# Attention scores of two heads at once: keys and queries transposed in float32 and split afterwards, scores as two 64-row tiles in three passes, one pool of PSUM banks

## The chip, the cores and the metric

The kernel runs on one core of a Trainium2 chip. The metric is the device time of one execution in microseconds (us). Five engines work side by side, each through its own instructions in a fixed order: TensorE (PE; its weight loads are listed apart as PEld), VectorE (DVE), ScalarE (ACT), GpSimd (POOL) and SyncE (SP), which issues most of the DMAs. TensorE writes only to PSUM, which the kernel uses as 8 banks of 128 partitions by 512 float32 values.

## The reference

```python
B, H, S, D = 4, 8, 576, 64
scores = np.matmul(q, k.transpose(0, 1, 3, 2)) / np.sqrt(D)
kth = np.partition(scores, -32, axis=-1)[..., -32:-31]        # the 32 largest of each row stay
scores = np.where(scores >= kth, scores, -1e9)
attn = softmax(scores)
x = (attn @ v)            # laid out as 2304 tokens of 512
# a mixture of experts on x: each token goes to the expert (of 8) with the largest logit
h = relu(x[mask] @ w1[e]); y[mask] = gate[mask] * (h @ w2[e])     # 512 -> 1024 -> 512
# a second block on y: SoLU, a normalization, and w_out
h = y @ w_in; s = h * softmax(h); out = normalize(s) * g_ln @ w_out
```

The scores must keep float32's exactness, since a row's 32nd largest decides which entries stay. A float32 value v is therefore written as hi + lo, where hi is v rounded to the type float32r, which TensorE multiplies in one pass, and lo is the rest; q.k is then a sum of products of such parts.

## The kernel before, in words

The kernel is one long program without loops on the chip. It is written as some twenty generators (load_k, load_q, prep_k_all, prep_q_all, attention with unit, pair and route, slots with front, backs with back and moe2, statics for the weights of the last block). Each yields its operations, with an engine and an estimated cost in ns, and takes and returns tokens of buffers ("get", "put"). A planner (class Order, L97) runs these against each other with the estimated costs and priorities (PRI, L35) and so fixes each engine's order of instructions before the program is built. On the chip every engine takes its instructions in that order; only the semaphores decide when.

Attention goes by batch b (4), tile t of queries (four of 128 rows, then one of 64) and pair p of heads (4). For the 128-row tiles a unit is one head (128 units), for the 64-row tile a unit is both heads of a pair, stacked as 128 rows (16 units).

- prep_kv (L481) makes a pair's keys ready: ACT copies the raw keys to hi (L486), POOL subtracts to lo (L487), TensorE transposes nine blocks of 128 by 128 in which hi and lo of one head lie side by side (L507), and ACT copies them out of PSUM in three pieces (L513). The result holds hi in partitions 0 to 63 and lo in 64 to 127.
- prep_q (L520) and turn_q (L535) do the same for queries: ACT (L527) and POOL (L528) split half a tile at a time, TensorE makes four transposes per pair (L543) and ACT copies each pair out (L549; for the 64-row tile L555, with zeros from POOL at L554). For one head there are two stationary operands of 128 rows: (hi, lo) and (lo, hi).
- unit (L563) makes the scores: both operands against the keys' (hi, lo), for two halves of 288 keys, so four matmuls of 128 rows and 288 columns a head (L579), eight for the stacked 64-row unit, in two PSUM banks. ACT copies both halves out (L586, L595), DVE takes the larger and the smaller of the halves (L597, L598) and then finds the 32nd largest by rounds of MAX8 and MATCH_REPLACE8 (L601 to L615). ACT and POOL make the masked exponentials (L632 to L636).
- pair (L645) transposes the exponentials (L668, L680, L683) and multiplies them with v (L702), in column tiles of 64.
- The experts are at L971 and L1002, the last block at L1023, L901 and L1084. A slot of 128 tokens becomes ready when enough rows of attention have been routed (PLAN, L53).

PSUM: all tiles share eight banks, and the planner hands them out by four kinds of token: pS = 2 for scores, T = 2 for transposes, O = 1 for the product with v, P = 3 for the last block and the experts. pS and O go to P when attention is done.

DMAs of k, q, v and the experts' weights are all issued by SP, in the planned order; an issue that waits for its buffer holds up those behind it. The buffer of raw keys (kr) and that of raw queries (qr) exist once each, transposed keys four times (kT), transposed queries twice (qT, one pair each).

Of the kernel before, what the change touches and what calls it, by code (L numbers as in the profile page):

```python
# [32 lines left out]
TUNE = dict(kr=1, qr=1, hl3=1, khl=1, kT=4, vt=6, qT=2, S=5, M=2, e=2, tops=5, eT=2, eT4=1, oT=1, xs=3, z=8, seq=1,  # L33
            row=2, xT=2, yT=4, tile=4, wraw=5, hh=2, tT=4, u=1, ot=2, pS=2, T=2, O=1, P=3, unit=7, pair=6)
# [9 lines left out]
OB = "O"  # L44
# [148 lines left out]
def attn_moe_solu_kernel(ctx, tc, q, k, v, mid, w_gate, mbias, w1, w2, w_in, w_out, g_ln, out):  # L193
# [12 lines left out]
    BUF = dict(kr=2, qr=2, hl3=1, khl=1, kT=4, vt=4, qT=3, S=SBUFS, M=2, e=3, tops=4, eT=2, eT4=1, oT=1, xs=2, z=8, seq=1,  # L206
               row=3, xT=2, yT=6, tile=4, wraw=6, ws=4, hh=2, tT=4, u=2, ot=2, pS=2, T=2, O=1, P=3, unit=UNITS, pair=2)
# [56 lines left out]
    def consts():  # L264


        yield "get", ("row", 2), ("xs", 1), ("T", 1)
# [40 lines left out]
        yield "put", ("T", 1)  # L308
# [57 lines left out]
    def static_w_in(kk, i, j):  # L366
# [4 lines left out]
        yield "get", ("P", 1)  # L371
# [4 lines left out]
        yield "put", ("P", 1)  # L376

    def static_w_out(kk, j):
# [3 lines left out]
        yield "get", ("P", 1 if pm else 2)  # L382
# [5 lines left out]
        yield "put", ("P", 1)  # L388
# [11 lines left out]
    def static_centre():  # L400
# [8 lines left out]
        yield "put", ("P", 1)  # L409
        done = [Ev() for _ in range(KF)]  # L410

        def centre(kk):
# [3 lines left out]
            yield "get", ("P", 1)  # L416
# [5 lines left out]
            yield "put", ("P", 1)  # L422
# [57 lines left out]

    def prep_kv(b, p):  # L481
        yield k_loaded[b, p]
        kr = kraw[b, p]
        yield "get", ("khl", 1)
        khl = sb.tile([128, 9, 2, D], F32R, tag="khl", name="khl", bufs=BUF["khl"])
        yield Op("ACT", 573, lambda: nc.scalar.activation(khl[:, :, 0, :], kr, AF.Copy))  # L486
        yield Op("POOL", 1360, lambda: nc.gpsimd.tensor_tensor(khl[:, :, 1, :], kr, khl[:, :, 0, :].bitcast(F32),  # L487
                                                               op=OP.subtract))
        yield "put", ("kr", 1)
# [10 lines left out]
        kt = sb.tile([128, 2, S], F32R, tag="kT", name="kT", bufs=BUF["kT"])  # L500
        for c0, c1 in ((0, 4), (4, 8), (8, 9)):
            yield "get", ("T", 1)
            pt = ps.tile([128, 4, 128], F32R, tag="B", name="pt", bufs=8)

            def tr():
                for c in range(c0, c1):
                    nc.tensor.transpose(pt[:, c - c0, :], khl[:, c, :, :].rearrange("p a d -> p (a d)"), identr)  # L507

            yield Op("PE", 60 * (c1 - c0), tr)
            at, w = ((0, 512), (640, 512), (512, 128))[c0 // 4]  # L510
            if c0 == 8:
                yield "put", ("khl", 1)
            yield Op("ACT", 478 if c0 < 8 else 157, lambda: nc.scalar.activation(  # L513
                kt.rearrange("p s n -> p (s n)")[:, at:at + w], pt[:, :c1 - c0].rearrange("p i n -> p (i n)").bitcast(F32), AF.Copy))
# [949 lines left out]
```

## Time and profile before

| | |
|---|---|
| three runs | 1073.13, 1073.67, 1076.36 us; median 1073.67 |
| the profiled execution | 1071.05 us, of which the span of its instructions is 1069.2 |
| busy over the span | PE 88%, PEld 75%, DVE 74%, ACT 68%, POOL 61% |
| chain that ended last | PE 56%, DVE 11%, DMA 9%, POOL 8%, ACT 5% |
| TensorE's granted clock, mean | 0.964 |

Busy is the share of the span in which an engine had an instruction under way; a matmul's end is modelled, and matmuls overlap, so a matmul's duration is longer than the distance from its start to the next one's. That distance is read from the starts in the timeline. The chain is followed back from the last instruction: at each step to what released it, or to the instruction before it on its engine. "x" is the number of instructions.

### The profile page before, as it was taken

The page shows a single profiled execution, that of the slowest core. Times are in us where ns is not written, and L with a number is a line of the kernel's source. Part 1 is how long each engine was busy: PE and PEld are TensorE (multiplying, and loading weights), DVE is VectorE, ACT ScalarE, POOL GpSimd, SP SyncE. Part 2 cuts the span into 40 slices and gives each one's busy share as a digit, 9 for nine tenths or more (in the row PEclk, how much of TensorE's full clock was granted, in tenths as well). Part 3 has the DMA queues.
Part 4 walks back from the last instruction along what each step waited for, and adds up shares of the span by engine and source line. Part 5 has one row for each costly group of instructions (what it writes and reads, how often), then busy time and mean ns, then how long its engine had stood idle before and what let it go on. Part 6 is the DMA issues. An engine that isn't in the chain of part 4 may idle for free.

```text
span 1069.2 us, 22944 instructions
## 1 busy us (share of the span) xinstructions
PE 942.3 (88%) x7230; PEld 800.8 (75%) x7230; DVE 787.9 (74%) x2717; ACT 731.9 (68%) x1798; POOL 649.5 (61%) x1397
## 2 busy tenths in 40 slices
PE   4677678988998989989999989999999979899993
PEld 3444456867887878878887878888888858788882
DVE  5988898975989989978899978888999721632111
ACT  5868676777787878868878767888787732533231
POOL 5768765775657767666677765766776534641111
PEclk9889898999999999989999989999999999999997
DMA  4443414336432434435433444244443337434530
GB/s 120 138 149 99 103 54 125 92 105 142 119 112 71 111 97 120 139 91 148 113 88 77 133 111 145 81 114 81 145 105 101 100 82 168 148 109 138 163 116 13
DMA packets 141243, 119.30 MB, mean 112 GB/s; under 512 B 31900, under 2 KB 113976, under 8 KB 141112
## 3 DMA queue, kind: packets, MB, share of 16 engines
q1 hardware_dynamic: 137016, 107.69, 37.6%
q0 software_dynamic: 4096, 10.05, 3.0%
q8 instruction: 59, 0.97, 0.4%
q14 instruction: 72, 0.59, 0.3%
HBM read 105.50 MB, written 12.21 MB: 110 GB/s over the span
## 4 chain that ended last, share of the span: by engine, by line
PE 56%; DVE 11%; DMA 9%; POOL 8%; ACT 5%; issue 4%; POOLq 0%; ACTq 0%; DVEq 0%
PE ph L971 10%; PE py L1002 9%; PE po L1084 8%; PE ph L1023 6%; DMA wraw<-in_moe_w_dram 6%; PE po L702 6%; PE pS L579 5%; PE pt L668 4%; DVE M L605 2%; POOL e L634 2%; PE pt L901 2%; PE pt L543 2%; DMA xg<-xrows,ids 2%; PE px L711 1%; DVE tops L608 1%
## 5 line engine op out<-in xcount | busy, mean ns | idle before, releaser
L634 POOL TENSOR_TENSOR e<-ss,e 128x576 f32<-128x576 f32 x144 | 206.3, 1436 | 52.1 <-ACT e L633 47.3
L605 DVE MATCH_REPLACE8 M<-tops,M 128x288 f32<-128x288 f32 x432 | 190.4, 442 | 0.0
L971 PE MATMUL ph<-xT,wraw 128*128 128x128 f32 x1088 | 152.5, 286 | 22.2 <-DMA wraw<-in_moe_w_dram 19.3
L971 PEld LDWEIGHTS ph<-xT,wraw 128*128 128x128 f32 x1088 | 138.5, 198 | 29.2 <-issue 13.1
L1002 PE MATMUL py<-hh,wraw 128*128 128x128 f32 x1088 | 147.4, 279 | 1.2 <-ACT hh L981 1.2
L636 ACT ACTIVATE e<-e,nb 128x576 f32<-128x576 f32 x144 | 112.1, 778 | 39.3 <-POOL e L634 38.4
L1002 PEld LDWEIGHTS py<-hh,wraw 128*128 128x128 f32 x1088 | 134.6, 193 | 5.4 <-issue 1.8
L579 PE MATMUL pS<-kT,qT 128*128 128x288 f32 x640 | 127.5, 326 | 10.3 <-ACT qT L549 9.0
L633 ACT ACTIVATE e<-ss,bt 128x576 f32<-128x576 f32 x144 | 111.0, 775 | 31.1 <-POOL bt L632 29.6
L608 DVE MAX8 tops<-M 128x8 f32<-128x288 f32 x288 | 128.5, 447 | 1.1
L702 PE MATMUL po<-eT,vt 128*64 128x128 f32 (+3 forms) x1600 | 115.2, 276 | 15.1 <-ACT eT L672 12.5
L1084 PE MATMUL po<-wo,lT 128*128 128x512 f32 x432 | 122.3, 420 | 3.6 <-ACT lT L905 2.1
L1023 PE MATMUL ph<-wi,yT 128*128 128x512 f32 x432 | 115.7, 407 | 2.0 <-ACT yT L1184 2.0
L702 PEld LDWEIGHTS po<-eT,vt 128*64 128x64 f32 (+1 forms) x1600 | 82.5, 138 | 43.7 <-ACT eT L672 15.8
L579 PEld LDWEIGHTS pS<-kT,qT 128*128 128x128 f32 x640 | 97.7, 199 | 21.1 <-ACT qT L549 9.6
L597 DVE TENSOR_TENSOR M<-pS,ss 128x288 f32<-128x288 f32 x144 | 64.4, 448 | 45.2 <-ACT ss L595 44.6
L672 ACT ACTIVATE eT<-pt 128x512 f32<-128x512 f32 (+1 forms) x160 | 88.2, 553 | 13.6 <-PE pt L668 12.2
L1084 PEld LDWEIGHTS po<-wo,lT 128*128 128x128 f32 x432 | 78.3, 195 | 21.6 <-DVE lT L909 3.0
L668 PE MATMUL pt<-identr,e 128*128 128x128 f32 (+1 forms) x640 | 92.6, 269 | 0.3 <-ACT ss L586 0.2
L1023 PEld LDWEIGHTS ph<-wi,yT 128*128 128x128 f32 x432 | 76.1, 188 | 20.9 <-ACT yT L1184 3.0
L981 ACT ACTIVATE hh<-ph 128x128 f32<-128x128 f32 (+1 forms) x144 | 40.1, 279 | 68.2 <-PE ph L971 67.6
L668 PEld LDWEIGHTS pt<-identr,e 128*128 128x128 f32 (+1 forms) x640 | 72.2, 142 | 11.4 <-issue 4.4
(218 smaller groups left out, 1951.4 us busy)
## 6 DMA issues: line engine op xcount, KB each, us to landing
wraw<-in_moe_w_dram SPq DMA_DIRECT2D x288, 256.0 KB
xrows<-xs SPq DMA_DIRECT2D x16, 288.0 KB
raw<-in_moe_w_out_dram SPq DMA_DIRECT2D x8, 512.0 KB
kr<-in_k_dram SPq DMA_DIRECT2D x32, 128.0 KB
qr<-in_q_dram SPq DMA_DIRECT2D x16, 256.0 KB
vt<-in_v_dram SPq DMA_DIRECT2D x32, 128.0 KB
raw<-in_moe_w_in_dram SPq DMA_DIRECT2D x8, 512.0 KB
wstage<-da SPq DMA_DIRECT2D x8, 256.0 KB
```

The costliest lines, as they stand in the source:

```text
L579: nc.tensor.matmul(pS[hf], w, kt[:, l, hf * HALF:(hf + 1) * HALF], start=i == 0, stop=i == 2 * len(srcs) - 1)
L605: nc.vector.match_replace(out=M, in_to_replace=rounds[r], in_values=M, imm_value=NEG)
L608: nc.vector.max(rounds[r + 1], M)
L633: yield Op("ACT", 667, lambda: nc.scalar.activation(e, ss, AF.Relu, bias=bt, scale=-BIG))
L634: yield Op("POOL", 1360, lambda: nc.gpsimd.tensor_tensor(e, ss, e, op=OP.subtract))
L636: yield Op("ACT", 760, lambda: nc.scalar.activation(e, e, AF.Exp, bias=nb, scale=0.125, accum_out=z))
L668: nc.tensor.transpose(pt[:, c, :], ef[r, at:at + 128], ident[r, r])
L702: nc.tensor.matmul(po[hs, :n], w, x, start=c == 0, stop=c == 4)
L971: nc.tensor.matmul(ph[:, :n], a[:, kk * 128:(kk + 1) * 128], b[:, kk, c0:c0 + n], start=kk == 0 and i == 0, stop=kk == KD - 1 and i == len ...
L1002: nc.tensor.matmul(py[c // k_][:, c % k_, :n], a[:, c * 128:(c + 1) * 128], b[:, :n], start=first and m == 0 and c % k_ == 0 and i == 0, s ...
L1023: nc.tensor.matmul(ph, y[a][:, kk, :], wi[b][:, kk, i * 512:(i + 1) * 512], start=kk == 0 and j == 0, stop=kk == KD - 1 and j == 2)
L1084: nc.tensor.matmul(po, l[a][:, c, :], wo[b][:, kk, :], start=kk == 0 and j == 0, stop=kk == KF - 1 and j == 2)
```

## The change

1. Keys (prep_kv): the load puts the two heads of a pair side by side, so that one float32 transpose turns 64 dimensions of both heads into 128 partitions: head 0 in 0 to 63, head 1 in 64 to 127. Four such transposes fill one bank and one more, of 64 rows, does the last 64 keys. The split comes after: ACT copies hi out of PSUM, DVE subtracts hi from PSUM and writes lo. The last 64 keys are written twice, ahead of and behind the 512, so that head 0 reads its 576 keys from column 64 and head 1 from column 0. The buffer of raw keys is returned after the last transpose; before, after the split.
2. Queries (prep_q): a whole tile, four pairs, in one bank by four float32 transposes, one split by ACT and DVE (for the 64-row tile two of each, and POOL writes the zeros). The buffer qT, still two, now holds a whole tile.
3. Scores (new function scores): for a 128-row tile both heads of a pair at once, as two 64-row tiles of the array, hi.hi, hi.lo and lo.hi: twelve matmuls in four banks. For the 64-row tile six matmuls of 128 rows in two banks. The second head's unit waits for the first one's operation.
4. PSUM tokens: one kind, B = 8, in place of pS, T, O and P. A token sc lets one pair at a time collect its banks.

```diff
-TUNE = dict(kr=1, qr=1, hl3=1, khl=1, kT=4, vt=6, qT=2, ..., pS=2, T=2, O=1, P=3, unit=7, pair=6)
+TUNE = dict(kr=1, qr=1, kT=4, vt=6, qT=2, ..., B=8, sc=1, unit=7, pair=6)
...
-                        nc.sync.dma_start(kr[:, 4 * s:4 * s + 4, :], k[b, 2 * p + s, 0:512].rearrange("(p c) d -> p c d", c=4))
-                    nc.sync.dma_start(kr[:, 8, :], k[b, 2 * p:2 * p + 2, 512:576, :])
+                        nc.sync.dma_start(kr[:, s:8:2, :], k[b, 2 * p + s, 0:512].rearrange("(p c) d -> p c d", c=4))
+                    nc.sync.dma_start(kr[0:64, 8:10, :], k[b, 2 * p:2 * p + 2, 512:576, :].rearrange("s p d -> p s d"))
...
+    def parts_of(hi, lo, pt, n):
+        yield Op("ACT", 55 + n * 833 // 1000, lambda: nc.scalar.activation(hi, pt, AF.Copy))
+        yield Op("DVE", 70 + n * 1042 // 1000, lambda: nc.vector.tensor_tensor(lo, pt, hi.bitcast(F32), op=OP.subtract))
...
     def prep_kv(b, p):
-        yield Op("ACT", 573, lambda: nc.scalar.activation(khl[:, :, 0, :], kr, AF.Copy))
-        yield Op("POOL", 1360, lambda: nc.gpsimd.tensor_tensor(khl[:, :, 1, :], kr, khl[:, :, 0, :].bitcast(F32), op=OP.subtract))
-        yield "put", ("kr", 1)
...
+        kt = sb.tile([128, 2, 640], F32R, tag="kT", name="kT", bufs=BUF["kT"])
+        yield "get", ("B", 1)
+        pt = ps.tile([128, 4, 128], F32, tag="B", name="pt", bufs=8)
+        def tr():
+            for c in range(4):
+                nc.tensor.transpose(pt[:, c, :], kr[:, 2 * c:2 * c + 2, :].rearrange("p s d -> p (s d)"), ident)
+        yield Op("PE", 440, tr)
+        yield from parts_of(kt[:, 0, 64:576], kt[:, 1, 64:576], pt.rearrange("p c n -> p (c n)"), 512)
+        yield "put", ("B", 1)
+        yield "get", ("B", 1)
+        pl = ps.tile([128, 64], F32, tag="B", name="pt", bufs=8)
+        yield Op("PE", 110, lambda: nc.tensor.transpose(pl, kr[0:64, 8:10, :].rearrange("p s d -> p (s d)"), ident[0:64, 0:64]))
+        yield "put", ("kr", 1)
+        ends = kt.rearrange("p a (e n) -> p a e n", n=64)[:, :, 0:10:9, :]
+        yield from parts_of(ends[:, 0], ends[:, 1], bc(pl, 2, 1), 128)
...
     def prep_q(b, t):
+        yield "get", ("qT", 1), ("B", 1)
+        x = qT[b, t] = sb.tile([128, 2, NP, 128], F32R, tag="qT", name="qT", bufs=BUF["qT"])
+        pt = ps.tile([128, NP, n], F32, tag="B", name="pt", bufs=8)
+        def tr():
+            for p in range(NP):
+                nc.tensor.transpose(pt[:, p, :], qr[:n, 2 * p:2 * p + 2, :].rearrange("p s d -> p (s d)"), ident[:n, :n])
+        yield Op("PE", 440, tr)
+        yield "put", ("qr", 1)
+        if n == 128:
+            yield from parts_of(x[:, 0], x[:, 1], pt, NP * n)
...
+    def scores(b, t, p):
+        n = rows_of(b, t)[1]
+        x, kt = qT[b, t], kT[b, p]
+        yield "get", ("sc", 1)
+        yield "get", ("B", 2)
+        if n == 128:
+            yield "get", ("B", 2)
+        bank = [[ps.tile([128, HALF], F32, tag="B", name="pS", bufs=8) for _ in range(2)] for _ in range(n // 64)]
+        yield "put", ("sc", 1)
+        def mm():
+            for i, (a, c) in enumerate(((0, 0), (0, 1), (1, 0))):
+                for hf in range(2):
+                    for s in range(n // 64):
+                        r = slice(64 * s, 64 * s + 64) if n == 128 else slice(0, 128)
+                        at = 64 * (1 - s) + hf * HALF
+                        nc.tensor.matmul(bank[s][hf], x[r, a, p, :], kt[r, c, at:at + HALF], start=i == 0, stop=i == 2)
+        yield Op("PE", 900, mm)
...
     def unit(b, t, p, s, abt, tht, u, no, done):
+        if not s:
+            yield q_ready[b, t]
+            yield kv_ready[b, p]
+            yield from scores(b, t, p)
+        yield scored[b, t, p]
+        pS = pS_[b, t, p][s or 0]
         yield "get", ("S", 1)
-        yield "get", ("pS", 2)
...
-        yield "put", ("pS", 2)
+        yield "put", ("B", 2)
```

Everywhere else "T", "O" and "P" in a get or a put become "B"; the two puts that gave pS and O to P at the end of attention are gone. In pair, the columns of the exponentials that are read for a 64-row tile start at 0 for both heads, since both now see their keys in one order.

## Rows read from the trace of the kernel before

**Rows 1.** Busy us by stretch (windows): stretch, length, each engine's busy time (instructions), PEclk, DMA share, GB/s.
```profile
0.00:175.00 175.00, 116.81 (x654) 79.13 (x654) 145.85 (x458) 126.52 (x285) 122.73 (x185) 0.91 0.39 111
175.00:850.00 675.00, 642.35 (x5332) 561.49 (x5333) 588.62 (x2115) 532.94 (x1349) 452.36 (x1025) 0.98 0.42 110
850.00:1069.00 219.00, 183.10 (x1245) 160.19 (x1245) 53.45 (x146) 72.43 (x165) 74.44 (x188) 0.96 0.42 118
```
**Rows 2.** PE's waits, 0 to 175 us: us in total, times, longest.
```profile
PE pt L507 <- POOL khl L487: 9.8, 2, 8.4
PE pS L579 <- ACT qT L549: 9.0, 3, 3.9
PE pt L543 <- POOL qhl L528: 5.5, 2, 3.5
```
**Rows 3.** DVE's longest wait, 175 to 850 us.
```profile
DVE M L597 <- ACT ss L595: 35.8, 39, 5.7
```
**Rows 4.** Groups by line on PE and PEld: instructions, busy us, mean ns, idle before.
```profile
L543 PE MATMUL pt<-identr,qhl 128*128 128x128 f32 x256 | 35.3, 265 | 5.5 <-POOL qhl L528 5.5
L543 PE MATMUL pt<-identr,qhl 64*128 64x64 f32 x64 | 8.0, 247 | 0.1
L507 PE MATMUL pt<-identr,khl 128*128 128x128 f32 x144 | 22.0, 269 | 9.8 <-POOL khl L487 9.8
L668 PEld LDWEIGHTS pt<-identr,e 64*128 64x128 f32 x128 | 10.3, 140 | 4.6 <-issue 2.4 <-ACT kT L513 0.3 <-ACT ss L586 0.2
```
**Rows 5.** PE's timeline around 424 us: start us, us, line, tiles, rows*columns of the array.
```profile
420.22 1.28 PE L579 MATMUL pS<-kT,qT 128*128 128x288 f32 x8
421.33 0.60 PE L668 MATMUL pt<-identr,e 128*128 128x128 f32 x4
421.86 0.50 PE L543 MATMUL pt<-identr,qhl 64*128 64x64 f32 x4
422.29 1.66 PE L1084 MATMUL po<-wo,lT 128*128 128x512 f32 x6
423.79 0.60 PE L668 MATMUL pt<-identr,e 128*128 128x128 f32 x4
424.22 1.06 PE L971 MATMUL ph<-xT,wraw 128*128 128x128 f32 x8
425.12 1.06 PE L1002 MATMUL py<-hh,wraw 128*128 128x128 f32 x8
425.93 0.54 PE L507 MATMUL pt<-identr,khl 128*128 128x128 f32 x4
426.30 1.29 PE L579 MATMUL pS<-kT,qT 128*128 128x288 f32 x8
```
**Rows 6.** PE's timeline around 455 us.
```profile
454.34 0.46 PE L668 MATMUL pt<-identr,e 64*128 64x64 f32 x4
454.73 1.16 PE L971 MATMUL ph<-xT,wraw 128*128 128x128 f32 x8
455.81 0.46 PE L711 MATMUL px<-iw,oT 128*64 128x144 f32 x2
```
**Rows 7.** PE's timeline in the 9 ns from 445.336 to 445.345 us.
```profile
445.34 0.33 PE L683 MATMUL pt<-identr,e 128*64 128x128 f32 x2
```
**Rows 8.** Groups by line on PE, 175 to 850 us: the scores.
```profile
L579 PE MATMUL pS<-kT,qT 128*128 128x288 f32 x536 | 100.7, 315 | 0.0
```
**Rows 9.** Groups by line on ACT.
```profile
L549 ACT ACTIVATE qT<-pt 128x512 fp32r<-128x512 f32 x64 | 38.3, 598 | 2.5 <-PE pt L543 2.2 <-PE pt L507 0.2
L527 ACT ACTIVATE qhl<-qr 128x512 fp32r<-128x512 f32 x32 | 20.4, 638 | 0.0
```
**Rows 10.** Groups by line on POOL.
```profile
L528 POOL TENSOR_TENSOR qhl<-qr,qhl 128x256 fp32r<-128x256 f32 x32 | 24.6, 768 | 8.5 <-ACT qhl L527 7.2 <-POOL nb L602 0.6
L487 POOL TENSOR_TENSOR khl<-kr,khl 128x576 fp32r<-128x576 f32 x16 | 23.1, 1445 | 10.9 <-ACT khl L486 10.6
```
**Rows 11.** A group by line on DVE: a subtraction of a full PSUM bank.
```profile
L909 DVE TENSOR_TENSOR lT<-pt,lT 128x512 fp32r<-128x512 f32 x36 | 24.6, 683 | 30.9 <-ACT lT L905 30.8
```

More of the change, by code (lines that the diff above doesn't have):

```diff
@@ L32 @@
 SBUFS = 3
-TUNE = dict(kr=1, qr=1, hl3=1, khl=1, kT=4, vt=6, qT=2, S=5, M=2, e=2, tops=5, eT=2, eT4=1, oT=1, xs=3, z=8, seq=1,
-            row=2, xT=2, yT=4, tile=4, wraw=5, hh=2, tT=4, u=1, ot=2, pS=2, T=2, O=1, P=3, unit=7, pair=6)
+TUNE = dict(kr=1, qr=1, kT=4, vt=6, qT=2, S=5, M=2, e=2, tops=5, eT=2, eT4=1, oT=1, xs=3, z=8, seq=1,
+            row=2, xT=2, yT=4, tile=4, wraw=5, hh=2, tT=4, u=1, ot=2, B=8, sc=1, unit=7, pair=6)
 PRI = {("ffn", "ACT"): 0.56, ("ffn", "DVE"): 0.46, ("ffn", "POOL"): 0.56, ("ffn", "SP"): 3.18, ("front", "ACT"): 2.49,
@@ L499, in prep_kv @@
         yield "get", ("kT", 1)
[L500 to L514, printed above, removed]
-            yield "put", ("T", 1)
+        kt = sb.tile([128, 2, 640], F32R, tag="kT", name="kT", bufs=BUF["kT"])
+        yield "get", ("B", 1)
+        pt = ps.tile([128, 4, 128], F32, tag="B", name="pt", bufs=8)
[4 more added lines that the diff above has]
+        yield from parts_of(kt[:, 0, 64:576], kt[:, 1, 64:576], pt.rearrange("p c n -> p (c n)"), 512)
+        yield "put", ("B", 1)
+        yield "get", ("B", 1)
+        pl = ps.tile([128, 64], F32, tag="B", name="pt", bufs=8)
[3 more added lines that the diff above has]
+        yield from parts_of(ends[:, 0], ends[:, 1], bc(pl, 2, 1), 128)
+        yield "put", ("B", 1)
         kT[b, p] = kt
@@ L522, in prep_q @@
         qr = qraw[b, t]
-        for g in range(2):
-            yield "get", ("hl3", 1)
-            hs = slice(4 * g, 4 * g + 4)
-            t_ = sb.tile([128, 4, 3, D], F32R, tag="hl3", name="qhl", bufs=BUF["hl3"])
-            yield Op("ACT", 500, lambda: nc.scalar.activation(t_[:n, :, 0:3:2, :], bc(qr[:n, hs], 2, 2), AF.Copy))
-            yield Op("POOL", 687, lambda: nc.gpsimd.tensor_tensor(t_[:n, :, 1, :], qr[:n, hs], t_[:n, :, 0, :].bitcast(F32),
-                                                                  op=OP.subtract))
-            if g:
-                yield "put", ("qr", 1)
-            yield from turn_q(b, t, t_, n, g)
-            yield "put", ("hl3", 1)
@@ new lines, in prep_q @@
+        yield Op("PE", 440, tr)
+        yield "put", ("qr", 1)
+        if n == 128:
+            yield from parts_of(x[:, 0], x[:, 1], pt, NP * n)
+        else:
+            for s in range(2):
+                z = x[64 * s:64 * s + 64, :, :, 64 * (1 - s):64 * (1 - s) + 64]
+                o2 = bc(bc(onesf[64 * s:64 * s + 64, :n], NP, 1), 2, 1)
+                yield Op("POOL", 900, lambda: nc.gpsimd.tensor_tensor(z, o2, o2, op=OP.subtract), deps=[])
+            for s in range(2):
+                r = slice(64 * s, 64 * s + 64)
+                yield from parts_of(x[r, 0, :, r], x[r, 1, :, r], pt[r], NP * n)
@@ new lines, in prep_q @@
+        yield "put", ("B", 1)
+        yield "set", q_ready[b, t]
+    E_, Z_, E_ready = {}, {}, {}
+    def scores(b, t, p):
[15 more added lines that the diff above has]
+        yield Op("PE", 900, mm)
+        pS_[b, t, p] = bank
+        if p == NP - 1:
+            yield "put", ("qT", 1)
+        if t == tiles(b)[-1]:
+            yield "put", ("kT", 1)
+        yield "set", scored[b, t, p]
@@ L570, in unit @@
+    def unit(b, t, p, s, abt, tht, u, no, done):
+        if not s:
[4 more added lines that the diff above has]
+        pS = pS_[b, t, p][s or 0]
         yield "get", ("S", 1)
         ss = sb.tile([128, S], F32, tag="S", name="ss", bufs=BUF["S"])
-        yield "get", ("pS", 2)
-        pS = [ps.tile([128, HALF], F32, tag="B", name="pS", bufs=8) for _ in range(2)]
-        def mm():
-            for i, (l, a) in enumerate((i, a) for i in srcs for a in range(2)):
-                w = x[:, l, a, :] if s is not None else x[:, a, l:l + 2, :].rearrange("p s n -> p (s n)")
-                for hf in range(2):
-                    nc.tensor.matmul(pS[hf], w, kt[:, l, hf * HALF:(hf + 1) * HALF], start=i == 0, stop=i == 2 * len(srcs) - 1)
```

116 lines of the change are left out of this document (38 added, 78 removed).

## The prediction

> **What bounds the kernel now.** I read the page's busy slices first, then cut the span at two places where the work changes and asked for busy time by stretch, then the waits of the two busiest engines, and last PE's timeline for distances between starts. The stretches are: up to 175 us, where attention runs alone beside the making of the last block's weights; 175 to 850, attention mixed with experts; 850 to the end, experts and the last block alone [rows 1]. In the middle stretch PE is busy 642.35 of 675 us, 95%, and DVE 588.62, 87%; ACT has 79%, POOL 67%. So PE is the bound there, with DVE close behind. DVE's largest wait in it is for scores, 35.8 us in 39 waits [rows 3]: ACT's copy of scores that PE delivered late. In the first stretch PE is busy 67%, DVE 83%, ACT 72%, POOL 70%; nothing is full, and PE waits 24.3 us (9.8 + 9.0 + 5.5) for the preparation of keys and queries [rows 2]. In the last stretch DVE has 24% and PE 84%; the change touches nothing in it but the names of bank tokens.
>
> **The change part by part, on PE.** Distances between starts, not durations, are PE's cost.
> Queries, 128-row tiles: 256 transposes before [rows 4], in 64 groups of four. A group of four such float32r transposes takes 425.93 to 426.30, 0.37 us [rows 5] (that row is of keys, the same form). 64 x 0.37 = 23.7 us. After, 16 groups of four float32 transposes; L668 shows four in 423.79 to 424.22, 0.43 us [rows 5]: 6.9 us. Saved 16.8.
> A switch of tile mode must be priced next. Four L668 followed by a 64-row operation take 421.33 to 421.86, 0.53 [rows 5], 0.10 more than without. Eight L971 between a 64-row operation and a 64-column one take 454.73 to 455.81, 1.08 [rows 6], against 0.90 (424.22 to 425.12 [rows 5]) where nothing switches: 0.18 for one switch, the first weight load uncovered included. I take 0.18 each way, 0.36 for an operation in another mode.
> Keys: 144 transposes before [rows 4], 16 x 9 x 0.0925 = 13.3 us. After, 16 x (0.43 + one transpose of 64 rows and half the columns, about 0.06, + 0.36) = 13.6. Nothing saved (-0.3).
> Queries, 64-row tiles: 64 transposes [rows 4] in 16 groups, each 421.86 to 422.29, 0.43 with the way out [rows 5], and some 0.19 of way in and uncovered load: 9.9 us. After, 4 groups of about 0.61: 2.4. Saved 7.5.
> Scores, 128-row tiles: 64 pairs of eight matmuls, 512 of 640 in all (the 64-row tiles have 16 x 8). Eight take 1.11 to 1.13 us [rows 5], 0.14 each, 71.7 us. After, twelve a pair. Whether the two 64-row tiles of a step run together is the main question, and no row has that form. The nearest: two 64-column matmuls of L683 start within 9 ns of each other [rows 7], so disjoint parts of the array do work at once. Bounds: all together, six steps of 0.14 and one switch each way, 1.20 us, 76.8 us in all, 5.1 more than before; one after the other, 12 x 0.14 + 0.36 = 2.04, 130.6 us, 58.9 more. I take the first, as the row is nearest to it.
> Scores, 64-row tiles: six for eight, 16 x 2 x 0.14 = 4.5 saved.
> Sum on PE: 16.8 - 0.3 + 7.5 - 5.1 + 4.5 = 23.4 us saved; at the other bound 30.4 lost. Of the 640 score matmuls 536 lie in the middle stretch [rows 8], 84%; by that share 19.7 us fall where PE is the bound.
>
> **DVE** takes over the subtraction. A full bank costs 0.683 us [rows 11]. Keys: 16 x (0.683 + a short one; between a quarter of that, 0.17, and all of it, I take 0.3) = 15.7. Queries: 16 x 0.683 = 10.9, and eight of half length (0.34 to 0.68, taken as 0.4), 3.2. Together 29.8 us more, 25 in the middle stretch: 588.6 + 25 = 614.
> **ACT and POOL** lose work: of L549 and L527, 58.7 us [rows 9], 16 copies of a bank remain, 9.6; POOL's 47.7 us of subtractions [rows 10] go, and zeros for four tiles come (eight operations of 512 values a partition, 512/576 of L487's 1.445, so 1.28 each, 10.3). Neither is the bound, so this counts only through queues: ACT's copies of scores and exponentials come a little sooner. I count nothing.
>
> **The middle stretch.** PE alone would make it 675 - 19.7 = 655. DVE would then be busy 614 of 655, 94%, with 41 us idle where it now has 86. It keeps up only if its waits shrink; the wait for scores (35.8 [rows 3]) should about halve, since the second head's scores come with the first's, and queries are ready a tile ahead. If DVE kept all its other idle time (86 - 18 = 68), the stretch would be 682. Between 655 and 682 I take 660: PE's order sets when DVE gets work, so its idle time is mostly slack. That is 15 saved.
>
> **The first stretch.** PE's three waits [rows 2] belong to steps that go: POOL's subtraction ahead of each transpose. In their place stand a float32 transpose straight from the load, ACT, DVE. The bounds are 0 (DVE, at 83%, gets some 5 us more) and 24.3; of the longest of them, 8.4, I take half, since the load must still land and the new chain runs through two engines as well: 4. **The last stretch** stays at 219.
>
> **Covers and queues.** The raw keys' buffer is now held until the last transpose, so the next pair's load is issued later, behind whatever SP waits for. The keys of successive pairs are needed two units apart, some 11 us (675 us for 84% of 144 units), and between a key buffer's release and its use stand up to four units of the 64-row tile, so I take a load that is 5 us late to be covered; uncovered it would cost DVE that much at each of three batch changes, 15 us. The key loads' pieces shrink from four rows of 64 values to one; the mean DMA share of 0.42 [rows 1] leaves room. In the planner's pool a pair's scores now hold four banks from PE's first matmul until DVE's two combining operations of the second head, where a unit held two; four remain for transposes, the product with v, experts and last block, which had six. I cost this at nothing because ACT empties a full bank in 0.598 us [rows 9], and name it below as a rival.
>
> **Sum.** 1071.05 - 15 - 4 = 1052 for an execution like the profiled one. The median of the runs is 2.6 higher, so 1055.
>
> **A rule against it.** Four 64-row transposes take 454.34 to 454.73, 0.39 us with the way out [rows 6], while one of their weight loads lasts 0.14 [rows 4]: four loads end to end, 0.56, do not fit, so loads in the same 64 rows do overlap the matmul before. The Trainium skill, TensorE: Matmul & The Clock Gate, section Part 3: Packing small matmuls, says in its list of what overlaps that a weight load overlaps a running matmul only where the row groups differ. By that rule every step of the new scores would show its load; this trace's row speaks against it, though for transposes, not for float32r products; its time is that of rival 1b.
>
> **The rivals.**
> 1. The tiles don't help. (a) The two run one after the other: 53.8 us more on PE than forecast (64 x 0.84), 45 in the middle stretch: 1100. For it: no row shows this form. Against: [rows 7]. 0.10. (b) They run together but every weight load is uncovered, at 0.08 a step (0.18 less the 0.10 of the switch alone): 64 x 6 x 0.08 = 31 more, 26 in the stretch: 1081. 0.07.
> 2. Banks, on the slower side: from the point where scores of two pairs are held at once, no bank is left for experts; PE, which is to fill its time with them, waits, and they are made up after 850, where PE is already at 84%. Priced at half of the idle PE now has in the middle stretch over again, 16, and the 15 not gained: about 1085. For: scores rank above experts in the order of getting banks. Against: only one pair collects at a time. 0.12.
> 3. DVE becomes the bound of attention: the stretch at 682, 1077, or up to 1080 with late keys. For: 94% needed of it. Against: 35.8 of its 86 us idle are a wait for PE's scores [rows 3]. 0.08.
> 4. Nothing measurable: PE's relief and DVE's load cancel, 1074. 0.09.
> 5. More than forecast: DVE's and PE's waits for each other shrink, half of PE's 32.6 us idle goes as well: 1055 - 16 = 1039, down to 1030 if the 24.3 us of [rows 2] go too. 0.14.
> The forecast, 1042 to 1069, has 0.40.
> Within 0.3%, about what a measurement here can tell from none, is 1070.5 to 1076.9. Faster: the forecast, rival 5 and 0.02 of rival 4, 0.56. Same: the rest of 4 and 0.03 of rival 3, 0.10. Slower: rivals 1 and 2 and the rest of 3, 0.34. The likeliest case's own range is 1042 to 1069; the range that takes in the others is 1032 to 1090, with 1a and the far end of 5 left out.
>
> **What would show it.** In the timeline of the changed kernel: starts of the two 64-row matmuls some ns apart and a pair's twelve in about 1.2 us (2.0 says rival 1a, 1.7 says 1b); four float32 transposes in 0.43 us, 16 + 16 groups of them; DVE's busy sum near 818 us and POOL's near 610; the middle stretch ending some 19 us earlier with PE still at 93% or more. PE idle in that stretch above 45 us with experts' matmuls waiting for ACT's copies says rival 2; DVE above 95% says rival 3. The forecast is wrong if a pair's scores take over 1.5 us, or if attention's last scores come no earlier.

## The result, and the profile after

The changed kernel takes 1058.85 us (median of 4 runs, 1055.57 to 1059.22) against 1073.4 (1070.32 to 1076.36) for the kernel before in the same series: ratio 0.9858, 95% interval 0.9824 to 0.9892. Measured again beside the second series of experiments it was 0.9892 (0.9845 to 0.9939). All ratios below are to the kernel before on the same chip. The forecast was 1055.

First the changed kernel's busy times, in the stretches of [rows 1] (columns as there; the last stretch ends with its span).

```profile
0.00:175.00 175.00, 123.01 (x682) 76.01 (x683) 149.61 (x472) 118.33 (x277) 108.28 (x167) 0.87 0.35 102
175.00:850.00 675.00, 624.18 (x5312) 525.11 (x5308) 598.78 (x2157) 490.22 (x1284) 426.88 (x1010) 0.98 0.45 112
850.00:1057.00 207.00, 176.63 (x1163) 157.24 (x1161) 47.85 (x125) 66.96 (x147) 64.58 (x160) 0.95 0.42 125
```

Second its page: busy sums, and the chain that ended last.

```profile
PE 923.8 (87%) x7150; PEld 758.4 (72%) x7150; DVE 796.2 (75%) x2752; ACT 675.5 (64%) x1706; POOL 599.7 (57%) x1335
...
PE 36%; DVE 22%; POOL 13%; DMA 9%; ACT 7%; issue 6%; SPq 0%; POOLq 0%; ACTq 0%; DVEq 0%
```

PE is busy 923.8 us, before 942.3: 18.5 less. The span went from 1069.2 to 1057.3, 11.9 less, so PE's idle time (span less busy) rose from 126.9 to 133.5. PE's part of the chain fell from 56% to 36%, and DVE's and POOL's rose from 11 and 8% to 22 and 13%: what ended last now runs more through a unit's steps on these two.

The last unit of attention is finished by a MAX8 that starts at 816.3 us; before, at 847.0 (DVE's timeline, first of the changed kernel, then of the kernel before):

```profile
816.25 0.18 DVE L621 MAX8 tht<-abt 128x8 f32<-128x16 f32 x1
846.96 0.16 DVE L615 MAX8 tht<-abt 128x8 f32<-128x16 f32 x1
```

That is 31 us earlier, but 19 of them are given back behind it: 241 us are left to the end, before 222. Of the experts' 2272 matmuls 1472 have started by then, before 1600. Their first one starts at 194.4 instead of 175.1; whether that is the cause is not shown. The kernel before with the pool alone (e3_before_pool below) starts its first at 176.9, ends attention at 811.7 and has 241 us left as well.

The new scores in PE's timeline (start, duration, line, tile), one pair:

```profile
508.79 0.39 PE L975 MATMUL ph<-xT,wraw 128*128 128x128 f32 x2
509.10 1.18 PE L571 MATMUL pS<-kT,qT 64*128 64x288 f32 x12
510.22 1.09 PE L708 MATMUL po<-eT,vt 128*64 128x128 f32 x16
```

From the first of the twelve to the next operation it is 1.12 us here, and 1.00 in the median of the 64 pairs; 1.20 was forecast. The two matmuls of a step start together, 4 ns apart, and a step begins some 0.13 us after the one before (0.24 after the first). PE's timeline in the 7 ns from 509.100 to 509.107 us has two of them:

```profile
509.10 0.40 PE L571 MATMUL pS<-kT,qT 64*128 64x288 f32 x2
```

The groups by line on PE (instructions, busy, mean ns, idle before) and of the new subtraction on DVE and copies on ACT:

```profile
L571 PE MATMUL pS<-kT,qT 64*128 64x288 f32 x768 | 80.7, 331 | 13.6 <-ACT eT L678 7.6 <-DVE m L604 1.9 <-ACT xs L723 1.5
L571 PE MATMUL pS<-kT,qT 128*128 128x288 f32 x96 | 16.9, 309 | 1.8 <-ACT eT L678 1.6 <-ACT hh L985 0.2
L533 PE MATMUL pt<-identr,qr 128*128 128x128 f32 x64 | 10.7, 294 | 15.7 <-DMA qr<-in_q_dram 15.4 <-DVE qT L483 0.2 <-ACT eT L678 0.2
L483 DVE TENSOR_TENSOR kT<-pt,kT 128x512 fp32r<-128x512 f32 x16 | 10.9, 682 | 3.4 <-ACT kT L482 3.4
L483 DVE TENSOR_TENSOR qT<-pt,qT 128x512 fp32r<-128x512 f32 x16 | 10.8, 678 | 12.5 <-ACT qT L482 12.5
L483 DVE TENSOR_TENSOR kT<-pt,kT 128x128 fp32r<-128x128 f32 x16 | 4.5, 279 | 1.7 <-ACT kT L482 1.6
L483 DVE TENSOR_TENSOR qT<-pt,qT 64x256 fp32r<-64x256 f32 x8 | 3.3, 413 | 0.1
L728 DVE TENSOR_TENSOR xs<-px,rz 128x144 f32<-128x144 f32 x24 | 7.1, 295 | 1.8 <-PE px L717 1.6 <-issue 0.2
L723 ACT ACTIVATE xs<-px,rz 128x72 f32<-128x72 f32 x80 | 21.1, 315 | 9.7 <-PE px L717 8.8 <-PE py L1006 0.8
```

The four rows of L483 sum to 29.5 us, 29.8 being forecast; yet DVE's busy sum rose by only 8.3. Part of the rest is the last two rows: the planner gives the scaled sums over heads to the less loaded engine, and 24 of them are on DVE instead of 41. So 5.0 us left DVE for ACT, which had lost work. The other 16 us are spread over many groups that the change doesn't name, none above 2.2.

### The profile page after: what moved, and what is told of

Same layout as the page of the kernel before. It is cut to its first block, busy times and chain, and to the rows that moved or that the text cites. A ratio compares the mean times of both kernels' runs of the same rounds, so it can differ in the third digit from the quotient of the medians.

```text
span 1057.3 us, 22609 instructions
## 1 busy us (share of the span) xinstructions
PE 923.8 (87%) x7150; PEld 758.4 (72%) x7150; DVE 796.2 (75%) x2752; ACT 675.5 (64%) x1706; POOL 599.7 (57%) x1335
## 4 chain that ended last, share of the span: by engine, by line
PE 36%; DVE 22%; POOL 13%; DMA 9%; ACT 7%; issue 6%; SPq 0%; POOLq 0%; ACTq 0%; DVEq 0%
PE py L1006 7%; PE ph L975 6%; DVE M L611 6%; PE po L1088 5%; PE ph L1027 5%; DMA wraw<-in_moe_w_dram 4%; PE po L708 3%; POOL e L640 3%; DVE tops L614 3%; PE pS L571 2%; PE pt L674 2%; DVE M L603 2%; DVE m L604 2%; DVE abt L614 2%; DVE tops L607 2%
## 5 line engine op out<-in xcount | busy, mean ns | idle before, releaser
L640 POOL TENSOR_TENSOR e<-ss,e 128x576 f32<-128x576 f32 x144 | 203.7, 1418 | 72.3 <-ACT e L639 69.3
L975 PE MATMUL ph<-xT,wraw 128*128 128x128 f32 x1088 | 147.7, 280 | 9.1 <-DMA wraw<-in_moe_w_dram 7.7
L975 PEld LDWEIGHTS ph<-xT,wraw 128*128 128x128 f32 x1088 | 135.4, 194 | 15.5 <-issue 7.1
L1088 PE MATMUL po<-wo,lT 128*128 128x512 f32 x432 | 121.2, 415 | 3.4 <-DVE lT L913 1.8
L571 PE MATMUL pS<-kT,qT 64*128 64x288 f32 (+1 forms) x864 | 97.5, 328 | 15.5 <-ACT eT L678 9.2
L571 PEld LDWEIGHTS pS<-kT,qT 64*128 64x128 f32 (+1 forms) x864 | 74.4, 197 | 36.0 <-ACT eT L678 10.6
L674 PE MATMUL pt<-identr,e 128*128 128x128 f32 (+1 forms) x640 | 95.6, 273 | 3.2 <-DVE xs L728 1.4
L1088 PEld LDWEIGHTS po<-wo,lT 128*128 128x128 f32 x432 | 76.7, 192 | 22.2 <-DVE lT L913 4.9
```

Source lines behind the costliest of these rows:

```text
L571: nc.tensor.matmul(bank[s][hf], x[r, a, p, :], kt[r, c, at:at + HALF], start=i == 0, stop=i == 2)
L640: yield Op("POOL", 1360, lambda: nc.gpsimd.tensor_tensor(e, ss, e, op=OP.subtract))
L674: nc.tensor.transpose(pt[:, c, :], ef[r, at:at + 128], ident[r, r])
L975: nc.tensor.matmul(ph[:, :n], a[:, kk * 128:(kk + 1) * 128], b[:, kk, c0:c0 + n], start=kk == 0 and i == 0, stop=kk == KD - 1 and i == len ...
L1088: nc.tensor.matmul(po, l[a][:, c, :], wo[b][:, kk, :], start=kk == 0 and j == 0, stop=kk == KF - 1 and j == 2)
```

## The experiments

**First series: is PE the bound, or DVE, or neither?** The first theory holds that the gain is PE's relief, the second that DVE has become the bound; the expectations say what each would give.

e1_serial: one head's six matmuls, then the other's. No other instruction changes its place.

```diff
-            for i, (a, c) in enumerate(((0, 0), (0, 1), (1, 0))):
-                for hf in range(2):
-                    for s in range(n // 64):
+            for s in range(n // 64):
+                for i, (a, c) in enumerate(((0, 0), (0, 1), (1, 0))):
+                    for hf in range(2):
```

> The changed kernel with its loop over the two heads of a pair moved outside, so that head 0's six matmuls come ahead of head 1's six and no two neighbours lie in different 64-row tiles. The order of every engine stays the same. Theory 1 (PE's time binds; the gain rests on the tiles running together): a pair's twelve matmuls, now 1.0 us, take 12 x 0.131 + 0.25 = 1.8, so PE gets 64 x 0.8 = 51 us more, of which 84% (43) in the stretch where it binds: about 1100 us (1085 to 1110). Theory 2 (DVE now sets the pace of attention and PE's order has slack): PE's idle takes most of it up, 1060 to 1075.

Ratio 0.9911 (0.9881 to 0.9940). A pair, in PE's timeline:

```profile
514.44 1.42 PE L571 MATMUL pS<-kT,qT 64*128 64x288 f32 x12
515.80 1.46 PE L708 MATMUL po<-eT,vt 128*64 128x128 f32 x20
```

It takes 1.36 us, in the median of the pairs 1.37 instead of 1.00. But the two tiles did not run one after the other. PE's timeline in the 7 ns from 514.440 to 514.447 us has one matmul, where the changed kernel has two:

```profile
514.44 0.40 PE L571 MATMUL pS<-kT,qT 64*128 64x288 f32 x1
```

The following starts are 0.24, 0.37, 0.375, 0.50, 0.61 and 0.63 us later. If a tile's own matmuls start 0.13 us apart, as in the changed kernel, two starts within 10 ns belong to different heads; the record names no head, so this is read from the distances. Read so, head 1 starts 0.375 us after head 0 and then runs beside it, and that delay is about all that the pair costs more. What one tile strictly after the other would cost, no run shows. PE is busy 948.5 us, 24.7 more than in the changed kernel (64 x 0.37 is 23.7), about half of the 51 that the expectation counted on. Scaled to that, theory 1 would make the time some 21 us longer than the changed kernel's; between the ratios, 0.9911 against 0.9858 and 0.9892, lie 2 to 6 us. PE's sum alone is not what sets the end of the changed kernel.

e2_light: DVE subtracts 8 columns of each operand only, and the scores' three products are all hi.hi, each overwriting the last (lo is left out of the result).

```diff
-nc.vector.tensor_tensor(lo, pt, hi.bitcast(F32), op=OP.subtract)
+nc.vector.tensor_tensor(lo[..., :8], pt[..., :8], hi.bitcast(F32)[..., :8], op=OP.subtract)
...
-nc.tensor.matmul(bank[s][hf], x[r, a, p, :], kt[r, c, at:at + HALF], start=i == 0, stop=i == 2)
+nc.tensor.matmul(bank[s][hf], x[r, 0, p, :], kt[r, 0, at:at + HALF], start=True, stop=True)
```

> The changed kernel with DVE's subtraction cut to the first 8 columns of each piece, and the three passes of the scores all reading the hi parts, each starting its sum anew, so the scores are hi.hi alone; PE's instructions, their order and that of all other engines stay the same. DVE loses 16 x 0.68 + 16 x 0.68 + 16 x 0.28 + 8 x 0.41 = 29.5 us less some 4 that the small pieces cost. Theory 1 (PE binds): within 4 us of the changed kernel's 1059, 1055 to 1059. Theory 2 (DVE binds attention since the change): 16 to 25 us less, 1034 to 1043.

Ratio 0.9891 (0.9829 to 0.9953), with DVE busy 777.3 us, 18.9 less: theory 2's 16 to 25 us are not there. DVE's subtraction costs nothing that can be measured.

e7_onepass: only hi.hi is computed, four matmuls a pair; the two other products are left out.

```diff
-            for i, (a, c) in enumerate(((0, 0), (0, 1), (1, 0))):
+            for i, (a, c) in enumerate(((0, 0),)):
...
-                        nc.tensor.matmul(bank[s][hf], x[r, a, p, :], kt[r, c, at:at + HALF], start=i == 0, stop=i == 2)
+                        nc.tensor.matmul(bank[s][hf], x[r, a, p, :], kt[r, c, at:at + HALF], start=True, stop=True)
```

> The changed kernel with one pass of the scores (hi.hi) in place of three; DVE's subtraction stays, its result is not read. The order stays the same. PE loses about 64 x 0.5 + 16 x 0.52 = 41 us. Theory 1 (PE binds): 25 to 35 us less than the changed kernel's 1059, 1024 to 1034. Theory 2 (DVE binds attention): under 10 less, 1049 to 1058.

Ratio 0.9840 (0.9797 to 0.9883): two thirds of the score matmuls gone, PE busy 907.6, and the gain over the changed kernel lies inside the intervals. PE's busy time fell by 16.2 us and not by the expectation's 41. The mean granted clock was lower, 0.935 (0.929 to 0.944 over the runs) against 0.960 in the changed kernel (0.949 to 0.962), so some 25 us of what was saved came back as slower matmuls, an estimate from these figures; PE idled 25.4 us more besides. The three runs say that in the changed kernel neither PE's nor DVE's busy sum alone sets the end. No run takes work from PE in the kernel before.

e3_before_pool: the kernel before with one kind of bank token, B = 8, for pS, T, O and P, and nothing else of the change.

```diff
-            row=2, xT=2, yT=4, tile=4, wraw=5, hh=2, tT=4, u=1, ot=2, pS=2, T=2, O=1, P=3, unit=7, pair=6)
+            row=2, xT=2, yT=4, tile=4, wraw=5, hh=2, tT=4, u=1, ot=2, B=8, unit=7, pair=6)
...
-        yield "get", ("pS", 2)
+        yield "get", ("B", 2)
```

> The kernel before with the one pool of 8 bank tokens alone; keys, queries and scores as before. Theory 1 (the pool costs and gives nothing, the gain is PE's): within 8 us of the kernel before, 1066 to 1081. Rival (the pool gives the gain, since bursts on any use get all banks): 1055 to 1064. Rival (the pool costs, and the new scores win more than shows): 1082 to 1095.

Ratio 0.9792 (0.9744 to 0.9840): the part that was costed at nothing gives, alone, at least what the whole change gives. Its windows:

```profile
0.00:175.00 175.00, 116.70 (x667) 79.11 (x668) 149.38 (x463) 129.92 (x292) 122.35 (x186) 0.91 0.37 111
175.00:850.00 675.00, 649.66 (x5444) 565.56 (x5443) 583.64 (x2133) 533.78 (x1365) 458.49 (x1059) 0.98 0.43 111
850.00:1052.00 202.00, 169.87 (x1123) 150.91 (x1121) 47.01 (x122) 64.62 (x143) 63.05 (x156) 0.96 0.43 125
```

Against [rows 1] PE does more in the middle stretch, 649.66 for 642.35 us, and so less is left after it. Of the 16.3 us that the span is shorter, 10.2 are PE's idle time, 116.7 us (1052.9 less 936.2) against 126.9, and 6.1 its busy time for the same matmuls.

**Second series: why the pool gains.** The theories' names stand in the first expectation.

again: the changed kernel.

> The changed kernel itself, unchanged, so that the next runs can be compared with it on one chip. Every theory expects its ratio to the kernel before again: 0.982 to 0.990.

0.9892 (0.9845 to 0.9939), as expected.

e4_split: the changed kernel, its banks divided up (the gets and puts name these tokens again).

```diff
-            row=2, ..., ot=2, B=8, sc=1, unit=7, pair=6)
+            row=2, ..., ot=2, pS=4, T=2, P=2, sc=1, unit=7, pair=6)
```

> The changed kernel with its banks divided up again: four for a pair's scores, two for transposes and the product with v, two for experts and last block (the four go to them when attention is done). The run of the kernel before with the pool alone had a ratio of 0.979, so the pool carries the gain; two theories say why. Theory S (scores ahead: with pS = 2 only one unit's scores could lie in PSUM, so PE couldn't make the next ones until DVE had combined these; with the pool two units' lie there): four banks for scores are kept here, so the gain stays, ratio 0.980 to 0.992. Theory F (free use: what counts is that transposes, the product with v and experts may take any bank): ratio 0.996 to 1.010. Theory N (chance: any new planned order lies somewhere within 1.5% of the old one, and no rule of banks stands behind it): no pattern with the next two runs.

0.9949 (0.9899 to 1.0000): between the two, nearer to F; its interval reaches into that of the run before (0.9845 to 0.9939).

e8_ps4: the kernel before, its banks divided up otherwise.

```diff
-            row=2, ..., ot=2, pS=2, T=2, O=1, P=3, unit=7, pair=6)
+            row=2, ..., ot=2, pS=4, T=2, P=2, unit=7, pair=6)
-OB = "O"
+OB = "T"
```

> The kernel before with its banks divided up otherwise and no pool: four for scores (two units), two for transposes and the product with v together, two for experts and last block. Theory S: ratio 0.975 to 0.986, as the pool alone gave. Theory F: 0.995 to 1.010, since the kinds that were to be freed have fewer banks than before. Theory N: somewhere from 0.975 to 1.005.

1.0149 (1.0097 to 1.0200), above what all three theories gave. Room for two units' scores, at the price of other banks, makes it slower; that speaks against S, but the banks taken from the others may hide a gain.

e9_pool_one: the pool, with one unit's scores at a time (shown against e3_before_pool).

```diff
+        yield "get", ("sc", 1)
         yield "get", ("B", 2)
...
-        yield "put", ("B", 2)
+        yield "put", ("B", 2), ("sc", 1)
```

> The kernel before with the one pool, but with one unit's scores in PSUM at a time, by a token that is held from the unit's first matmul to DVE's two combining operations. Theory S: the gain is gone, ratio 0.995 to 1.005. Theory F: the gain stays, 0.975 to 0.986. Theory N: somewhere from 0.975 to 1.005.

0.9792 (0.9746 to 0.9839), the same as e3_before_pool, in another order. With one unit's scores at a time the gain is still there, so S is out. F fits this run, and N too; on this chip e9_pool_one (1055.91 us, 1051.96 to 1060.27) was also faster than the changed kernel (1065.44, 1064.37 to 1071.87). It and e3_before_pool are the fastest versions measured.

**Third series: how much is chance of the planned order?**

e10_before_cost: the kernel before; the planner assumes 560 ns for a unit's scores.

```diff
-        t1 = yield Op("PE", 510 * len(srcs), mm)
+        t1 = yield Op("PE", 560 * len(srcs), mm)
```

> The kernel before, with the cost that the planner assumes for a unit's scores put up from 510 to 560 ns and nothing else; only the planned order changes. It measures chance. Theory F (the pool's free use of banks carries the gain): 0.990 to 1.010, away from the 0.979 of both kernels with a pool. Theory N (any new order may give as much): as likely as not below 0.985.

1.0097 (1.0062 to 1.0131), inside F's range; an order alone moved the kernel before by 1%.

e12_to: in the kernel before, transposes and the product with v share three tokens.

```diff
-            row=2, ..., ot=2, pS=2, T=2, O=1, P=3, unit=7, pair=6)
+            row=2, ..., ot=2, pS=2, T=3, P=3, unit=7, pair=6)
-OB = "O"
+OB = "T"
```

> The kernel before with one small piece of the pool: transposes and the product with v share three tokens (before two and one), scores keep two, experts and last block three. If the piece that PE lacks is a bank for attention's own chain of transposes and products, the gain is here: 0.976 to 0.986. If it is that experts and attention lend each other banks, nothing: 0.993 to 1.007. Theory N: anywhere from 0.975 to 1.010.

0.9902 (0.9874 to 0.9930), between the two expectations. It is half of the pool's gain, but no more than the 1% by which the run before moved. After attention the kernel before has six banks for experts and last block, this one five, since the third token stays with the transposes.

e6_cost: the changed kernel; the planner assumes 1000 ns for a pair's scores.

```diff
-        yield Op("PE", 900, mm)
+        yield Op("PE", 1000, mm)
```

> The changed kernel with the planned cost of a pair's scores put up from 900 to 1000 ns (1.0 us is what the trace shows for them); only the order changes. If the 1% by which the changed kernel (0.9858, again 0.9892) stays behind the pool alone (0.979) belongs to its waits and not to one order, this one too lies at 0.984 to 0.994. If it is chance, 0.975 to 0.983 is as likely.

1.0139 (1.0102 to 1.0176): outside both expectations. The same instructions in another order (7150 on PE in both), and the changed kernel is slower than the kernel before. One cost estimate moves this kernel by 1.0139/0.9892, 2.5%, more than the whole change did.

What the order does is seen in its windows of 5 us around 385 us:

```profile
375.00:380.00 5.00, 4.23 (x47) 3.24 (x45) 5.00 (x20) 3.92 (x9) 2.33 (x9) 1.00 0.17 62
380.00:385.00 5.00, 1.86 (x21) 1.19 (x21) 4.92 (x17) 4.19 (x11) 4.10 (x12) 0.89 0.00 0
385.00:390.00 5.00, 3.43 (x9) 2.29 (x10) 5.00 (x19) 3.59 (x10) 3.40 (x10) 0.50 0.00 0
390.00:395.00 5.00, 5.00 (x19) 3.94 (x18) 5.00 (x20) 2.23 (x5) 2.25 (x5) 0.59 0.00 2
395.00:400.00 5.00, 5.00 (x50) 4.59 (x50) 2.89 (x11) 4.42 (x12) 1.82 (x3) 1.00 0.30 93
```

From 380 to 385 PE is busy 1.86 of 5 us; DVE is full. Then the granted clock is 0.50, its lower level of 1.2 GHz, and stays there for part of the next 5 us, in which PE is busy throughout. The 19 matmuls there and the 50 at 1.00 are not of one kind; ten of the 19 are of the last block's L1088, 512 columns wide (PE's timeline):

```profile
389.49 4.63 PE L1088 MATMUL po<-wo,lT 128*128 128x512 f32 x10 [0.20 <-DVE lT L913]
393.92 0.69 PE L674 MATMUL pt<-identr,e 128*128 128x128 f32 x4
```

They take 4.43 us, 0.44 each, where six of the same form take 1.50 us, 0.25 each, in the kernel before at a granted clock of 1.00 (422.29 to 423.79 [rows 5]). So a hole costs more than its length. Over the span, e6_cost is 35.7 us longer than the changed kernel (1093.0 to 1057.3); 23.2 of them are PE's busy time for the same matmuls (947.0 to 923.8, mean clock 0.936 to 0.960) and 12.5 are idle.

e14_early: e6_cost, with DVE combining both halves from SBUF.

```diff
-        tM = yield Op("DVE", 369, lambda: nc.vector.tensor_tensor(M, pS[1], ss[:, :HALF], op=OP.max), deps=[t0])
-        tm = yield Op("DVE", 369, lambda: nc.vector.tensor_tensor(m, pS[1], ss[:, :HALF], op=OP.min), deps=[t0])
         yield "put", ("B", 2)
+        tM = yield Op("DVE", 369, lambda: nc.vector.tensor_tensor(M, ss[:, HALF:], ss[:, :HALF], op=OP.max))
+        tm = yield Op("DVE", 369, lambda: nc.vector.tensor_tensor(m, ss[:, HALF:], ss[:, :HALF], op=OP.min))
```

> The kernel of the last run (1000 ns) with DVE's two combining operations reading both halves of the scores in SBUF, so that a unit's banks come back after ACT's two copies and not after DVE. If the four banks that a pair's scores hold are what takes the new scores' gain away again, this gains 0.8 to 1.5% on the last run (ratio 0.972 to 0.982). If it is PE's waits for ACT's copies in the chain from the product with v to the sum over heads, nothing changes or DVE waits longer for the second copy: 0.984 to 1.000.

1.0795 (1.0728 to 1.0861), 6.5% above e6_cost, which neither theory expected. The two combining operations, first of e6_cost, then of e14_early (busy us, mean ns):

```profile
L603 DVE TENSOR_TENSOR M<-pS,ss 128x288 f32<-128x288 f32 x144 | 64.1, 445 | 15.7 <-ACT ss L601 14.4
L604 DVE TENSOR_TENSOR m<-pS,ss 128x288 f32<-128x288 f32 x144 | 63.8, 443 | 0.0
```

```profile
L604 DVE TENSOR_TENSOR M<-ss 128x288 f32<-128x288 f32 x144 | 86.9, 606 | 22.4 <-ACT ss L601 22.2
L605 DVE TENSOR_TENSOR m<-ss 128x288 f32<-128x288 f32 x144 | 101.7, 706 | 0.0
```

They cost 60.7 us more. The timeline of e14_early (start, duration) shows why:

```profile
30.16 1.41 POOL L640 TENSOR_TENSOR e<-ss,e 128x576 f32<-128x576 f32 x1 [2.18 <-ACT e L639]
30.42 1.46 DVE L605 TENSOR_TENSOR m<-ss 128x288 f32<-128x288 f32 x1
...
192.13 1.40 POOL L640 TENSOR_TENSOR e<-ss,e 128x576 f32<-128x576 f32 x1
...
192.72 1.12 DVE L604 TENSOR_TENSOR M<-ss 128x288 f32<-128x288 f32 x1
```

DVE's operation ends 0.31 us after POOL's both times (31.88 and 31.57; 193.84 and 193.53): it waits for POOL's product of two SBUF operands to end. 67 of the 288 take over 0.6 us, and 66 of these end 0.31 to 0.33 us after an instruction of POOL, 59 of them after this product. With one operand in PSUM nothing of the kind is seen: all of e6_cost's 288 take 429 to 460 ns. The Trainium skill, GPSIMD Engine Reference, section 1. Specifications, says that GpSimd shares its SBUF interfaces with VectorE and contends with VectorE's instructions that have two SBUF inputs; these rows agree. So this run measured that stall and not the banks' earlier return: whether the four held banks cost anything stays open.

All profiles together. PE idle is the span less PE's busy sum; the column before the last is 636 us less PE's busy time from 175 to 811 us (attention ends at 811.7 in e3_before_pool).

| run | scores | ratio | span us | PE busy us | PE idle us | idle 175 to 811 | mean clock |
|---|---|---|---|---|---|---|---|
| before | old | 1 | 1069.2 | 942.3 | 126.9 | 32.5 | 0.964 |
| e3_before_pool | old | 0.9792 | 1052.9 | 936.2 | 116.7 | 22.6 | 0.966 |
| e9_pool_one | old | 0.9792 | 1053.5 | 937.2 | 116.3 | 22.7 | 0.960 |
| e12_to | old | 0.9902 | 1066.9 | 941.7 | 125.2 | 34.5 | 0.956 |
| e10_before_cost | old | 1.0097 | 1083.0 | 954.4 | 128.6 | 27.4 | 0.950 |
| e8_ps4 | old | 1.0149 | 1098.8 | 955.6 | 143.2 | 53.6 | 0.952 |
| changed kernel | new | 0.9858 | 1057.3 | 923.8 | 133.5 | 49.5 | 0.960 |
| again | new | 0.9892 | 1062.6 | 923.9 | 138.7 | 52.2 | 0.960 |
| e2_light | new | 0.9891 | 1061.6 | 930.8 | 130.8 | 48.0 | 0.954 |
| e1_serial | new, serial | 0.9911 | 1071.3 | 948.5 | 122.8 | 41.9 | 0.959 |
| e7_onepass | new, a third | 0.9840 | 1066.5 | 907.6 | 158.9 | 69.6 | 0.935 |
| e4_split | new | 0.9949 | 1076.8 | 934.2 | 142.6 | 49.8 | 0.950 |
| e6_cost | new | 1.0139 | 1093.0 | 947.0 | 146.0 | 49.9 | 0.936 |
| e14_early | new | 1.0795 | 1168.4 | 971.9 | 196.5 | 92.5 | 0.915 |

Two things are read from it. With the new scores PE idles 42 to 52 us in the middle, whatever the order and the tokens (e7_onepass and e14_early, which alter a pair's work, more); with the old it idles 22 to 35, e8_ps4 apart. So part of the work that PE lost came back as waiting: over the whole span 6.6 us of idle time for 18.5 of work against the kernel before, and against the pool alone (e3_before_pool) 16.8 for 12.4. And e7_onepass, where PE loses more, waits more. And within either kind one cost estimate of the planner moves the time, by 1.0% with the old scores (e10_before_cost) and 2.5% with the new (e6_cost against again).

## Why the prediction was right in its number, and where its reasons failed

The number is right, and in part by luck: the sum took 15 us from PE's relief in the middle and nothing from the pool, while the pool alone gives 2.1%, some 22 us, and the rest adds nothing to that in the orders tried.

- *Scores run together*: right. The two matmuls of a step start 4 ns apart, and a pair takes 1.00 us in the median for 1.20. Rivals 1a and 1b did not come; how large 1a would have been stays open, since e1_serial did not force it. For 1b, a tile's matmuls start 0.13 us apart in the changed kernel, while one of their weight loads has a median of 184 ns, so loads into the same rows do overlap the matmul before, for float32r products as well. The rule that the prediction cites from the Trainium skill (TensorE: Matmul & The Clock Gate, Part 3: Packing small matmuls), that a weight load overlaps a running matmul only where the row groups differ, does not hold here.
- *PE's work*: 18.5 us less busy, 23.4 forecast, about right in the sum. Its term for the scores was mis-sized: the groups of eight in [rows 5] are units of the 64-row tile, and those of the 128-row tiles come in fours that take 0.625 us in the median, 80 us for 128 of them and not 71.7. So by these distances the new scores save 16 us (64 x 1.00 after) where 5.1 more were forecast. Four float32 transposes take 0.44 us in the median for 0.43.
- *DVE +29.8*: measured 29.5 for the new operations. The busy sum, forecast near 818, came to 796.2: the planner's own balance was not counted. *POOL near 610*: 599.7. *DVE's wait for scores halves* [rows 3]: 17.9 us from 175 to 811, before 34.4 there, right.
- *Middle stretch, 675 to 660, because PE is the bound there*: this is the step that failed. PE at 95% was read as the bound, so that it stays full and work taken from it shortens the stretch. But from 175 to 811 us it idles 49.5 us, before 32.5, and the kernel with the pool alone, whose PE has 12.4 us more to do, is not slower (span 1052.9 for 1057.3). In the changed kernel, taking work from PE (e7_onepass) or giving it some (e1_serial) hardly moves the time, and DVE relieved (e2_light) doesn't either. That PE was not the bound of the kernel before either is inferred; a likely reason, not shown by a run, is that it is filled with experts' work that can wait. Attention did end 31 us earlier, but more of the experts' work was left, and in the middle PE is busy 92.5%, not 93 or more. The forecast's mark for rival 2, over 45 us of idle PE, was passed too (50.8 of the 675), but not by the pool: with the banks divided (e4_split) PE idles as long. The rows of PE's waits from 175 to 811 us, first of the changed kernel, then of e3_before_pool (total, times, longest), show where: attention's own chain from the product with v over ACT's copy to the sum over heads, and weights.

```profile
PE px L717 <- ACT oT L715: 10.0, 14, 2.3
PE py L1006 <- DMA wraw<-in_moe_w_dram: 4.9, 3, 3.1
PE pt L905 <- DMA xg<-xrows,ids: 4.7, 2, 3.3
PE po L708 <- ACT eT L678: 4.2, 4, 1.6
PE ph L975 <- DMA wraw<-in_moe_w_dram: 3.7, 2, 3.4
```

```profile
PE ph L969 <- DMA wraw<-in_moe_w_dram: 5.6, 1, 5.6
PE px L711 <- ACT oT L709: 4.4, 9, 0.9
PE pt L899 <- DMA xg<-xrows,ids: 3.3, 2, 2.5
PE po L702 <- ACT eT L672: 2.2, 3, 1.5
```

- *First stretch, 4 us gained*: wrong. Units finished by 175 us: 24 before and after. In place of the waits of [rows 2] stands a new one, the first row here (PE's waits, 0 to 175 us, changed kernel):

```profile
PE pt L533 <- DMA qr<-in_q_dram: 15.4, 2, 7.8
PE px L717 <- ACT oT L715: 10.7, 6, 3.9
```

  The buffer of raw queries exists once, and the second load is issued at 13.63 us; its transposes stand ahead of the first scores in PE's order, so these start at 18.70 us, before at 17.24.
- *Last stretch, unchanged at 219*: 207 us remained after 850, but attention now ends 34 us ahead of that cut, before 3; counted from attention's end it grew by 19 us.
- *The pool, nothing*: wrong, and in sign the opposite of rival 2. Both kernels with the pool alone lie at 0.9792, below all four others with old scores (0.9902 to 1.0149). With the scatter of order that e10_before_cost and e6_cost show, two against four makes the pool likely as the source of a gain; it does not prove it.

What is shown: in these versions the planned order moves the time more than an engine's busy sum does (2.5% by one estimate and the same instructions, under 1% by 16 to 25 us of PE's or DVE's sum); the pool in the two orders that it produced gains 2.1%; the other parts, on top of it, did not gain in the orders tried (0.9858 and 0.9892 with all parts, 0.9792 with the pool alone). What stays open: what the new scores are worth in a planned order as good as the old one's. Each version here had one to three orders, and their scatter is as large as the difference.

## What to carry to other kernels

Where a planner fixes every engine's order, a change of costs, tokens or sizes is first of all a new order: perturb an estimate in both kernels, and take as the change's effect only what exceeds that scatter. An engine at 95% need not be the bound when it is filled with work that can wait; what bounds is found by removing its work and looking whether the end moves, and whether the granted clock moved with it. Of a change with several parts, run the part that was costed at nothing by itself.

## What was not expected of the hardware

- Two 64-row tiles of the array, fed in turn, take twelve products of 288 columns in 1.00 us (median). With one head's six ahead of the other's in the program it is 1.37: the second head's matmuls then start 0.375 us after the first's and, as the distances between starts read, beside them.
- After 5 us in which PE was busy 1.86 us, the granted clock was 0.50 and 0.59 in the next two stretches of 5 us, the second with PE busy throughout; products of 512 columns took 0.44 us each meanwhile, against 0.25 at 1.00.
- Some DVE operations with both operands in SBUF (67 of 288) stood still until POOL's instruction, mostly its product of two SBUF operands, had ended: up to 2.28 us for an operation of 0.44.
